# The gate of a feed-forward layer: from one VectorE instruction to one of ScalarE and two of GpSimd, with other block sizes in one pair of batches

## The chip, the core and the metric

The kernel runs on one core of a Trainium2 chip. A core has five engines with queues of their own, each in order: TensorE (PE in the profile; its weight loads are shown apart as PEld), VectorE (DVE), ScalarE (ACT), GpSimd (POOL) and SyncE (SP), which here issues the DMAs. TensorE writes its products to PSUM; the other data lie in SBUF. The metric is the device time of one execution in microseconds, lower being better; a kernel's time is the median of several executions.

## What is computed

Top-k attention, and behind it a feed-forward layer with an ELU gate, on 8 batches of 576 rows and 8 heads of 64:

```python
# attention: q, k, v of (8, 8, 576, 64), float32
scores = scale * np.matmul(q, k.transpose(0, 1, 3, 2))
kth = np.partition(scores, -top_k, axis=-1)[..., -top_k:-top_k + 1]   # top_k = 32
mask = scores >= kth
scores = np.where(mask, scores, -1000000000.0)
scores = scores - np.max(scores, axis=-1, keepdims=True)
attn = np.exp(scores)
attn = attn / (np.sum(attn, axis=-1, keepdims=True) + 1e-09)
attn_out = np.matmul(attn, v)
...
# feed-forward: x is attn_out as (4608, 512); w_in (512, 2048), w_out (2048, 512)
h = x @ w_in
g = np.where(h > 0.0, h, alpha * (np.exp(np.minimum(h, 0.0)) - 1.0))  # alpha = 1
out = g @ w_out
```

The weights come as 64-bit floating-point numbers and are decoded to 32 bits on the core.

## The kernel before

**Tiles and steps.** The 576 query rows of a batch are four tiles of 128 and one of 64; the 64-row tiles of two batches share one slot of the feed-forward layer. So a pair of batches has nine slots of 128 rows. One *step* is one query tile with two heads (for 64-row tiles, four half-filled heads); there are 144 steps, 18 to a batch. The main loop goes over the steps, and what it issues in step n belongs to several of them: `scores` of step n+2, `select` of step n, `mask` and `normalise` of step n-1, `turn` of step n-2, `attend` of a group whose last step is turned.

- `scores` (L273, L281): TensorE multiplies queries by keys into PSUM, ScalarE copies the scaled product to SBUF (`sc`).
- `select` (L291 to L301): for each of the two heads VectorE takes the eight largest values, replaces them by a very small number, and does so until the 32nd largest is known: four MAX8 and three MATCH_REPLACE8 over 576 columns.
- `mask` (L315 to L319): GpSimd makes `neg` and `gap` from the 32nd and the first maximum; ScalarE drops what is under the 32nd with a steep Prelu, and takes Exp, with the sum over a row.
- `normalise` (L328 to L332): GpSimd adds the epsilon (`dene`), VectorE takes the reciprocal (`rec`), GpSimd multiplies the rows.
- `turn` (L348, L349): TensorE transposes the weights into PSUM in two pieces of four 128-column chunks and one of one; ScalarE copies them to `et`. PSUM has two buffers for this and for the products of `attend`.
- `attend` (L375, L399): the product with the values, copied by ScalarE into `xT`, the transposed input of the feed-forward layer. `xT` has two buffers.

**Feed-forward blocks.** Slots are put together in blocks; a block can start when all of its slots are attended. For each of 16 chunks of 128 hidden units, `hidden` multiplies the block's tokens (128, 256 or 384 columns, by the number of slots) with four pieces of `w_in` into a PSUM bank (`hps`, L429). The gate is computed as max(h, exp(min(h, 0)) - 1): ScalarE forms n = Relu(-h) (L437) and n = Exp(-n) (L438), and VectorE takes n - 1 and the maximum with h, from PSUM, in one SCALAR_TENSOR_TENSOR (L409), which writes `gT`. This last instruction is put on a list, `gates`, and issued by `close_gates` at the next call of `feed`, before a third chunk, or before a `project`. Then `project` multiplies a slot's 128 columns of `gT` with `w_out` (L447), in four parts of four matmuls; ScalarE copies the result (L456), and SyncE stores it (L459). `hps` and the product of `project` share two PSUM banks.

**Order of the work.** The pieces of all blocks stand in one list, `ffn`. `feed` is called four times a step and takes pieces off the list at a pace worked out from the blocks' due times: work that must be done before the next block comes is spread evenly. A piece's cost in this sum is `HIDDEN` (by the number of slots) or `PROJECT`. The order on each engine is set when the program is built; the layer that builds it can interleave instructions where their dependencies allow it, so that, for instance, the two heads of a step stand mixed in VectorE's queue. During the first steps `hook` also decodes the weights (L151 to L186), on SyncE, VectorE, ScalarE and GpSimd.

**Divisions.** The first pair of batches has blocks of 1, 1, 2, 1, 2 and 2 slots, the other three pairs of 2, 2, 3 and 2. The 64-row slot (`rest`) lies in the three-slot block.

Of the kernel before, what the change touches and what calls it, by code (L numbers as in the profile page):

```python
# [8 lines left out]
AF = mybir.ActivationFunctionType  # L9
ALU = mybir.AluOpType  # L10
FP32 = mybir.dt.float32
# [4 lines left out]
TAKEN = -1.0e30  # L16
EPS = 1.0e-9
STEEP = 1.0e30
HIDDEN = {1: 1.1, 2: 1.85, 3: 2.7}
PROJECT = 3.55  # L20


# [57 lines left out]
def kernel(  # L80
# [9 lines left out]
    nc = tc.nc  # L90
    P = nc.NUM_PARTITIONS
    B, H, S, D = q.shape
# [8 lines left out]
    NG = NF // 2  # L101
    T = 3 * P
    scale = 1.0 / float(D) ** 0.5
# [3 lines left out]
    def pool(name, bufs, **kw):  # L107
        return ctx.enter_context(tc.tile_pool(name=name, bufs=bufs, **kw))
# [6 lines left out]
    etpool = pool("et", 2)  # L115
    small = pool("small", 4)
    xtpool = pool("xt", 2)
    fpool = pool("f", 2)
    opool = pool("o", 1)
    ps_sc = pool("ps_sc", 1, space=PSUM)  # L120
    ps_t = pool("ps_t", 2, space=PSUM)
# [279 lines left out]
        if blk.left == 0:  # L401
            ffn.extend(ffn_pieces(blk))

    gates = []

    def close_gates():
        for dst, n, ps in gates:
            w = dst.shape[-1]
            nc.vector.scalar_tensor_tensor(  # L409
                out=dst, in0=n[:, 0:w], scalar=-1.0, in1=ps[:, 0:w],  # L410
                op0=ALU.add, op1=ALU.max,
            )
        gates.clear()

    def ffn_pieces(blk):
        n_tok = blk.slots * P

        def hidden(f):
            if f == 0 and blk.number == 0:
                g = early.tile([P, NF, P], FP32, tag="g", name="gT")  # L420
                blk.gT = [g[:, 0:NG], g[:, NG:NF]]
            elif f % NG == 0 and blk.number > 0:
                g = late["g"].tile([P, NG, T], FP32, tag="g", name="gT")
                blk.gT.append(g[:])
            if len(gates) > 1:
                close_gates()
            ps = ps_f.tile([P, dm], FP32, tag="f", name="hps")
            for i in range(NC):
                nc.tensor.matmul(  # L429
                    ps[:, 0:n_tok],  # L430
                    w_in[:, i, f * P : (f + 1) * P],
                    blk.xT[:, i, 0:n_tok],
                    start=(i == 0),
                    stop=(i == NC - 1),
                )
            n = fpool.tile([P, T], FP32, tag="n", name="n")
            nc.scalar.activation(n[:, 0:n_tok], ps[:, 0:n_tok], AF.Relu, scale=-1.0)  # L437
            nc.scalar.activation(n[:, 0:n_tok], n[:, 0:n_tok], AF.Exp, scale=-1.0)  # L438
            gates.append((blk.gT[f // NG][:, f % NG, 0:n_tok], n, ps))

        def project(s, part):
            close_gates()
            if part == 0:
                blk.o = ps_f.tile([P, dm], FP32, tag="f", name="ops")
            step = NF // 4
            for f in range(part * step, (part + 1) * step):
                nc.tensor.matmul(  # L447
                    blk.o[:],
                    blk.gT[f // NG][:, f % NG, s * P : (s + 1) * P],
                    w_out[:, f, :],  # L450
                    start=(f == 0),
                    stop=(f == NF - 1),
                )
            if part == 3:
                o = opool.tile([P, dm], FP32, tag="osb", name="osb")
                nc.scalar.copy(o[:], blk.o[:])  # L456
                for t in blk.tiles[s]:
                    p0 = t.cols.start - s * P
                    nc.sync.dma_start(out[t.rows, :], o[p0 : p0 + t.ql, :])  # L459

        part = HIDDEN[blk.slots]
        behind = 2 * NF if blk.number else 0
        return [
            (part, max(behind, NC * (f // 4 + 1)), lambda f=f: hidden(f))
            for f in range(NF)
        ] + [
            (PROJECT, max(behind, NF + (part + 1) * NF // 4),
             lambda s=s, part=part: project(s, part))
            for s in range(blk.slots)
            for part in range(4)  # L470
        ]
# [4 lines left out]
    for b in range(B):  # L476
        if b % 2 == 0:
            rest = 2 * J
            division = [(0,), (1,), (2, 3), (rest,), (4, 5), (6, 7)]
            if b > 0:  # L480
                division = [(0, 1), (2, 3), (rest, 4, 5), (6, 7)]
            slots = {}
            for part in division:
                blk = Block(len(blocks), len(part))
                blocks.append(blk)
                slots.update((x, (blk, s)) for s, x in enumerate(part))
        first[b] = len(steps)
        tiles = []
        for qt in range(J + 1):
            r0 = b * S + (JP if qt == J else qt)  # L490
            if qt == J:
                (blk, slot), c0, n = slots[rest], (b % 2) * R, R
                rows = slice(r0, r0 + R)
            else:
                (blk, slot), c0, n = slots[(b % 2) * J + qt], 0, P
                rows = slice(r0, r0 + J * (P - 1) + 1, J)
            c0 += slot * P
            t = Tile(b, qt, rows, blk, slice(c0, c0 + n))
            blk.left += NHP
            blk.tiles[slot].append(t)  # L500
            tiles.append(t)
        order = [(0, 1), (2, 3), (J,)] if b % 2 == 0 else [(0, 1), (J,), (2, 3)]
        if b == 0:
            order[:1] = [(0,), (1,)]
        for qts in order:
            for hp in range(NHP // 2 if qts == (J,) else NHP):
                group = Group([tiles[qt] for qt in qts], hp)
                steps += [Step(tiles[qt], hp, group, i) for i, qt in enumerate(qts)]
            for qt in qts:
                n = len(steps)  # L510
                tiles[qt].block.ready = n + 1.0 if n <= tight else n + 2.5
    NS = len(steps)
    total = 0.0
    for blk in sorted(blocks, key=lambda x: x.ready):
        due.append((blk.ready, total))
        total += NF * HIDDEN[blk.slots] + 4 * blk.slots * PROJECT

# [5 lines left out]
    for b in range(1, B):  # L523
        f = first[b]
# [8 lines left out]

    def feed(n, share):

        close_gates()
        fed["at"] = max(fed["at"], n)
        ahead = [(w - fed["sum"]) / (x - fed["at"]) for x, w in due if x > fed["at"]]
        if ahead:
            fed["over"] += max(0.0, share * min(ahead))  # L540
        fed["at"] += share
        while ffn and decoded[0] >= ffn[0][1] and 0.5 * ffn[0][0] <= fed["over"]:
            cost, _, piece = ffn.pop(0)
            fed["over"] -= cost
            fed["sum"] += cost
            piece()
# [26 lines left out]
    for n in range(NS + 3):  # L573
# [5 lines left out]
        if n < tight:  # L579
            for i in range(2):  # L580
                passes = choose(n, i)
                next(passes)
                if i == 0:
                    while closing:
                        attend(closing.pop(0))
                elif prev:
                    normalise(prev)
                    turn(prev, slice(0, J))
                    turn(prev, slice(J, J + 1))
                    turn(prev, slice(J + 1, 2 * J + 1))  # L590
                feed(n, 0.25)
                next(passes)
                mask(cur, i)
                feed(n, 0.25)
            continue
        if prev:
            mask(prev, 0)
        passes = choose(n, 0)
        next(passes)
        feed(n, 0.25)  # L600
        while closing:
            attend(closing.pop(0))
# [15 lines left out]
        feed(n, 0.25)  # L618
    while ffn:
        ffn.pop(0)[2]()  # L620
    close_gates()


# [31 lines left out]
```

## Time and profile before

| what | value |
|---|---|
| median of 5 runs | 1872.49 us (1871.59 to 1872.92) |
| the profiled execution, its own time | 1872.64 us |
| the profiled execution, span of the core | 1870.8 us |
| mean granted TensorE clock | 0.952 |
| VectorE, MAX8 of 576 columns (L291, L301) | 754 and 757 ns, 1152 of them |
| VectorE, MATCH_REPLACE8 (L295) | 749 ns, 864 of them |
| VectorE, gate (L409) by 128, 256, 384 columns | 285, 414, 546 ns; 48, 192, 48 of them |
| ScalarE, Relu from PSUM (L437) by the same | 276, 380, 484 ns |
| ScalarE, Exp (L438) by the same | 310, 416, 524 ns |
| TensorE, passes of `hidden` (L429) by the same | 320, 389, 504 ns; 384, 1536, 384 of them |
| TensorE, passes of `project` (L447) | 606 ns, 1152 of them |

An engine's busy time is the union of its instructions' spans. A float32 matmul stands in the records as two passes; passes overlap, and their ends are modelled, so the mean of one pass is longer than the distance between two in a row. A wait in the profile is idle time of an engine before an instruction, put down to what released it: "A <- B: total us, times, longest". The lists of groups give busy time, mean ns of one, and idle time before them. A row of the windows gives a stretch of the span, then for each engine its busy time and number of instructions, the granted clock, and the DMA's share and rate.

### The profile page before, as it was taken

The page shows a single profiled execution, that of the slowest core. Times are in us where ns is not written, and L with a number is a line of the kernel's source. Part 1 is how long each engine was busy: PE and PEld are TensorE (multiplying, and loading weights), DVE is VectorE, ACT ScalarE, POOL GpSimd, SP SyncE. Part 2 cuts the span into 40 slices and gives each one's busy share as a digit, 9 for nine tenths or more (in the row PEclk, how much of TensorE's full clock was granted, in tenths as well). Part 3 has the DMA queues.
Part 4 walks back from the last instruction along what each step waited for, and adds up shares of the span by engine and source line. Part 5 has one row for each costly group of instructions (what it writes and reads, how often), then busy time and mean ns, then how long its engine had stood idle before and what let it go on. Part 6 is the DMA issues. An engine that isn't in the chain of part 4 may idle for free.

```text
span 1870.8 us, 25844 instructions
## 1 busy us (share of the span) xinstructions
PE 1714.9 (92%) x8352; PEld 1032.6 (55%) x8352; DVE 1605.1 (86%) x3408; ACT 1144.0 (61%) x2505; POOL 442.6 (24%) x1080
## 2 busy tenths in 40 slices
PE   5457999999999999999999999999998999899999
PEld 3235656565665565655546464655546466555555
DVE  7989999999999998989989888988989888898400
ACT  6777667666666665757557575656656565665421
POOL 3776222222222211221221212221221212121100
PEclk8556999999999999999999999999999999999999
DMA  6421011001100101001100011001100000000000
GB/s 162 137 102 68 19 26 45 6 7 47 42 7 1 31 22 47 1 25 27 44 12 1 25 26 44 7 6 38 39 18 7 19 19 26 6 7 6 1 18 12
DMA packets 101126, 56.20 MB, mean 30 GB/s; under 512 B 84096, under 2 KB 92288, under 8 KB 100992
## 3 DMA queue, kind: packets, MB, share of 16 engines
q1 hardware_dynamic: 100992, 54.55, 10.5%
q8 instruction: 67, 1.10, 0.2%
q14 instruction: 67, 0.55, 0.1%
HBM read 45.09 MB, written 9.44 MB: 29 GB/s over the span
## 4 chain that ended last, share of the span: by engine, by line
DVE 61%; PE 21%; ACT 11%; issue 3%; POOL 1%; DMA 1%; SPq 0%; POOLq 0%; ACTq 0%; DVEq 0%
DVE wk L295 25%; DVE m L301 22%; PE hps L429 8%; DVE m L291 8%; PE ops L447 6%; ACT sc L318 3%; DVE gT L409 3%; ACT sc L319 3%; PE scps L273 3%; ACT sc L281 2%; PE avps L375 2%; PE eps L348 2%; DVE raw L168 1%; DMA raw<-in_moe_w_in_dram 1%; DVE raw L182 1%
## 5 line engine op out<-in xcount | busy, mean ns | idle before, releaser
L301 DVE MAX8 m<-wk 128x8 f32<-128x576 f32 x864 | 632.1, 757 | 4.6
L429 PE MATMUL hps<-xT,w_in 128*128 128x256 f32 (+2 forms) x2304 | 576.0, 397 | 38.0 <-DVE gT L409 37.8
L447 PE MATMUL ops<-w_out,gT 128*128 128x512 f32 x1152 | 536.9, 606 | 0.0
L429 PEld LDWEIGHTS hps<-xT,w_in 128*128 128x128 f32 x2304 | 407.9, 198 | 154.3 <-DVE gT L409 59.9
L295 DVE MATCH_REPLACE8 wk<-m,wk 128x576 f32<-128x576 f32 x576 | 430.2, 749 | 0.0
L318 ACT ACTIVATE sc<-sc,neg 128x576 f32<-128x576 f32 x288 | 223.4, 776 | 273.5 <-POOL neg L315 272.2
L447 PEld LDWEIGHTS ops<-w_out,gT 128*128 128x128 f32 x1152 | 209.0, 193 | 207.2 <-issue 201.2
L349 ACT COPY et<-eps 128x512 f32<-128x512 f32 (+1 forms) x432 | 193.5, 475 | 151.5 <-PE eps L348 151.4
L273 PE MATMUL scps<-kqT 64*128 64x64 f32 (+3 forms) x1280 | 258.0, 463 | 14.0 <-ACT sc L281 13.3
L348 PE MATMUL eps<-ident,sc 128*128 128x128 f32 x1296 | 207.9, 284 | 55.2 <-POOL sc L332 17.6
L315 POOL TENSOR_SCALAR neg<-m 128x1 f32<-128x1 f32 x288 | 62.9, 219 | 819.9 <-DVE m L301 819.3
L348 PEld LDWEIGHTS eps<-ident,sc 128*128 128x128 f32 x1296 | 161.1, 145 | 172.0 <-issue 61.3
L332 POOL TENSOR_SCALAR sc<-sc,rec 128x576 f32<-128x576 f32 x288 | 214.2, 754 | 137.9 <-DVE rec L330 132.4
L291 DVE MAX8 m<-sc 128x8 f32<-128x576 f32 x288 | 210.8, 754 | 29.1 <-ACT sc L281 27.2
L319 ACT ACTIVATE sc<-sc,gap 128x576 f32<-128x576 f32 x288 | 223.2, 775 | 16.1 <-ACT sc L318 0.7
L375 PE MATMUL avps<-et,vT 128*64 128x256 f32 (+5 forms) x2000 | 205.8, 338 | 13.7 <-ACT et L349 13.4
L295 DVE MATCH_REPLACE8 wk<-m,sc 128x576 f32<-128x576 f32 x288 | 214.5, 749 | 0.0
L409 DVE SCALAR_TENSOR_TENSOR gT<-n,hps 128x256 f32<-128x256 f32 (+2 forms) x288 | 119.2, 414 | 107.1 <-ACT n L438 105.8
L437 ACT ACTIVATE n<-hps 128x256 f32<-128x256 f32 (+2 forms) x288 | 109.3, 380 | 151.6 <-PE hps L429 150.4
L273 PEld LDWEIGHTS scps<-kqT 64*128 64x128 f32 (+1 forms) x1280 | 117.8, 184 | 136.0 <-issue 112.1
L281 ACT ACTIVATE sc<-scps 128x576 f32<-128x576 f32 x288 | 170.6, 640 | 12.4 <-PE scps L273 12.3
L375 PEld LDWEIGHTS avps<-et,vT 128*64 128x64 f32 (+1 forms) x2000 | 114.4, 140 | 102.9 <-issue 41.1
(38 smaller groups left out, 807.9 us busy)
## 6 DMA issues: line engine op xcount, KB each, us to landing
kin<-in_k_dram SPq DMA_DIRECT2D x64, 128.0 KB, 2.8
qin<-in_q_dram SPq DMA_DIRECT2D x64, 128.0 KB, 2.9
raw<-in_moe_w_in_dram SPq DMA_DIRECT2D x16, 512.0 KB, 4.4
vT<-in_v_dram SPq DMA_DIRECT2D x64, 128.0 KB, 2.3
raw<-in_moe_w_out_dram SPq DMA_DIRECT2D x16, 512.0 KB, 3.2
out_dram<-osb SPq DMA_DIRECT2D x32, 256.0 KB, 2.2
kin<-in_k_dram SPq DMA_DIRECT2D x32, 32.0 KB, 2.5
qin<-in_q_dram SPq DMA_DIRECT2D x32, 32.0 KB, 2.5
```

The lines of the kernel that those rows point to most:

```text
L273: nc.tensor.matmul(ps[rows, start[i] : start[i] + keys.stop - keys.start], kq[part, 1, q0 : q0 + u.t.ql], kq[part, 0, keys], start=True, s ...
L281: nc.scalar.activation(u.sc[:, i, :], ps[:, first[i] : first[i] + S], AF.Copy, scale=scale)
L291: nc.vector.max(m, sc)
L295: nc.vector.match_replace(wk[:], m, cur, TAKEN)
L301: nc.vector.max(m, cur)
L318: nc.scalar.activation(sc, sc, AF.Prelu, bias=neg[:], alpha=STEEP)
L319: nc.scalar.activation(sc, sc, AF.Exp, bias=gap[:], accum_out=u.den[:, i : i + 1])
L332: nc.gpsimd.tensor_scalar(u.sc[:, i, :], u.sc[:, i, :], rec[:, i : i + 1], 1.0, ALU.mult, ALU.mult)
L348: nc.tensor.transpose(ps[:, c * P : (c + 1) * P], sc[:, c0 : c0 + P], ident[:])
L375: nc.tensor.matmul(ps[i * D : (i + 1) * D, cols], vt[rows, 2 * J if c == J else i * J + c, :], w, start=(c == 0), stop=(c == J),)
L429: nc.tensor.matmul(ps[:, 0:n_tok], w_in[:, i, f * P : (f + 1) * P], blk.xT[:, i, 0:n_tok], start=(i == 0), stop=(i == NC - 1),)
L447: nc.tensor.matmul(blk.o[:], blk.gT[f // NG][:, f % NG, s * P : (s + 1) * P], w_out[:, f, :], start=(f == 0), stop=(f == NF - 1),)
```

## The change

VectorE no longer takes part in the gate. The gate is computed as Relu(h) + (Exp(-Relu(-h)) - 1): ScalarE reads the PSUM bank twice, once for Relu(-h) into `n` and once for Relu(h) directly into `gT`, and takes Exp of `n`; GpSimd subtracts one from `n` and adds it to `gT`. `gates` and `close_gates` are gone. The buffer of `n` has three copies instead of two. The pair of batches 4 and 5 is divided into three blocks of three slots; pairs 2-3 and 6-7 keep theirs, as does the first. The costs by which `feed` paces the work are changed for two and three slots.

```diff
-HIDDEN = {1: 1.1, 2: 1.85, 3: 2.7}
+HIDDEN = {1: 1.1, 2: 1.92, 3: 2.68}
...
-    fpool = pool("f", 2)
+    fpool = pool("f", 3)
...
-    gates = []
-
-    def close_gates():
-        for dst, n, ps in gates:
-            w = dst.shape[-1]
-            nc.vector.scalar_tensor_tensor(
-                out=dst, in0=n[:, 0:w], scalar=-1.0, in1=ps[:, 0:w],
-                op0=ALU.add, op1=ALU.max,
-            )
-        gates.clear()
...
-            if len(gates) > 1:
-                close_gates()
...
-            n = fpool.tile([P, T], FP32, tag="n", name="n")
-            nc.scalar.activation(n[:, 0:n_tok], ps[:, 0:n_tok], AF.Relu, scale=-1.0)
-            nc.scalar.activation(n[:, 0:n_tok], n[:, 0:n_tok], AF.Exp, scale=-1.0)
-            gates.append((blk.gT[f // NG][:, f % NG, 0:n_tok], n, ps))
+            n = fpool.tile([P, T], FP32, tag="n", name="n")[:, 0:n_tok]
+            g = blk.gT[f // NG][:, f % NG, 0:n_tok]
+            nc.scalar.activation(n, ps[:, 0:n_tok], AF.Relu, scale=-1.0)
+            nc.scalar.activation(g, ps[:, 0:n_tok], AF.Relu)
+            nc.scalar.activation(n, n, AF.Exp, scale=-1.0)
+            nc.gpsimd.tensor_scalar_add(n, n, -1.0)
+            nc.gpsimd.tensor_tensor(g, g, n, ALU.add)
...
             division = [(0,), (1,), (2, 3), (rest,), (4, 5), (6, 7)]
             if b > 0:
+                division = [(0, 1, 2), (3, 4, 5), (rest, 6, 7)]
+            if b in (2, B - 2):
                 division = [(0, 1), (2, 3), (rest, 4, 5), (6, 7)]
```

The calls of `close_gates` in `project`, in `feed` and at the kernel's end are removed as well.

## The prediction

> **What bounds the kernel now.** I read first the page's busy shares and the chain that ended last, then the engines' busy time by stage, the gate's rows, the waits, and a stretch of the timeline.
>
> ```profile
> PE 1714.9 (92%) x8352; PEld 1032.6 (55%) x8352; DVE 1605.1 (86%) x3408; ACT 1144.0 (61%) x2505; POOL 442.6 (24%) x1080
> ...
> DVE 61%; PE 21%; ACT 11%; issue 3%; POOL 1%; DMA 1%; SPq 0%; POOLq 0%; ACTq 0%; DVEq 0%
> ```
>
> The chain lies mostly on VectorE, yet TensorE is busier. So the stages have to be told apart. I cut the span where the weights are decoded (212 us), where TensorE's load rises (664) and where the last selections end (1741): stages A to D.
>
> ```profile
> 0.00:212.00 212.00, 135.12 (x551) 82.28 (x552) 185.24 (x358) 148.27 (x302) 117.69 (x147) 0.66 0.34 103
> 212.00:664.00 452.00, 437.48 (x2343) 273.92 (x2343) 437.70 (x973) 304.49 (x695) 103.97 (x298) 0.99 0.10 25
> 664.00:1741.00 1077.00, 1017.02 (x5021) 604.92 (x5018) 962.13 (x2035) 657.92 (x1434) 218.52 (x628) 0.99 0.08 20
> 1741.00:1871.00 130.00, 125.28 (x443) 71.52 (x441) 20.08 (x44) 33.33 (x76) 2.43 (x7) 1.00 0.03 11
> ```
>
> Columns after the length: PE, PEld, DVE, ACT, POOL busy. B has both engines at 437 of 452. C has PE at 1017 and DVE at 962 of 1077. D is TensorE alone. The same cut for the gate, L409, on DVE in B and C:
>
> ```profile
> 212.00:664.00 452.00, 32.46 (x88) 0.99 0.10 25
> 664.00:1741.00 1077.00, 71.79 (x161) 0.99 0.08 20
> ```
>
> In A it is 4.35 and in D 10.57 us. The waits of stage C, DVE's and PE's, and two of the whole span:
>
> ```profile
> DVE rec L330 <- POOL dene L328: 64.4, 29, 2.8
> ```
> ```profile
> PE hps L429 <- DVE gT L409: 20.0, 19, 1.9
> ```
> ```profile
> POOL neg L315 <- DVE m L301: 819.3, 267, 8.6
> ...
> ACT sc L318 <- POOL neg L315: 272.2, 161, 5.3
> ```
>
> DVE's 29 waits for `dene` are one loop, seen once in the timeline:
>
> ```profile
> 1259.05 0.76 DVE L301 MAX8 m<-wk 128x8 f32<-128x576 f32 x1
> ...
> 1259.98 0.21 POOL L315 TENSOR_SCALAR neg<-m 128x1 f32<-128x1 f32 x1 [1.95 <-DVE m L301]
> ...
> 1260.22 0.78 ACT L318 ACTIVATE sc<-sc,neg 128x576 f32<-128x576 f32 x1 [0.58 <-POOL neg L315]
> 1261.09 0.78 ACT L319 ACTIVATE sc<-sc,gap 128x576 f32<-128x576 f32 x1
> ...
> 1262.31 0.17 DVE L330 RECIPROCAL rec<-dene 128x2 f32<-128x2 f32 x1 [2.50 <-POOL dene L328]
> ```
>
> The last maximum of a step goes to GpSimd, through ScalarE twice, back to GpSimd and to the reciprocal, which stands next in VectorE's queue: 2.5 us of nothing. So in C VectorE's own side is 962 + 64 = 1026 of 1077, TensorE's 1017. In B they are 437.7 + 2.7 and 437.5 of 452. Two engines are level, and 3 to 5% goes into waiting on each other.
>
> **The change, part by part.**
>
> *Gate off VectorE.* 288 instructions leave (119.2 us in the page's group): 4.4 in A, 32.5 in B, 71.8 in C, all on an engine that sets the pace there; 10.6 in D lies beside TensorE and is worth nothing. The waits of DVE for `n` (13.4 us in C, 10.2 in B) go with them.
>
> *One more Relu on ScalarE.* The blocks of the middle pair become 3+3+3 instead of 2+2+3+2, so hidden chunks are 48 of 128, 144 of 256 and 80 of 384 columns. Priced by the existing Relu from PSUM (0.276, 0.380, 0.484 us):
>
> ```profile
> L437 ACT ACTIVATE n<-hps 128x256 f32<-128x256 f32 x192 | 73.0, 380 | 95.3 <-PE hps L429 95.0
> ```
>
> 13.2 + 54.7 + 38.7 = 107 us; the fewer instructions of the other two give back 6. ACT goes from 1144 to 1245 us, in C from 61 to about 68%. It stays off the limit, but it is in order: behind a Relu stand the mask's Prelu and Exp and the copies that free PSUM for the transposes.
>
> *Two new instructions on GpSimd.* No two-input row of this width exists there. Bounds from these:
>
> ```profile
> L332 POOL TENSOR_SCALAR sc<-sc,rec 128x576 f32<-128x576 f32 x288 | 214.2, 754 | 137.9 <-DVE rec L330 132.4 <-PE qkps L245 1.7 <-PE eps L348 1.3
> ...
> L317 POOL TENSOR_TENSOR gap<-m,m 128x1 f32<-128x1 f32 x288 | 56.7, 197 | 0.4
> ...
> L177 POOL TENSOR_TENSOR raw<-raw 128x512 f32<-128x512 f32 x32 | 43.7, 1366 | 18.2 <-ACT raw L170 18.1
> ```
>
> The scalar add lies between 0.219 us (L315, one column) and 0.754 (576 columns), the tensor add between 0.197 and 1.366. On straight lines between them, by width, a 256-column pair costs 0.45 + 0.78 = 1.23 us; all of them 126 + 221 = 347 us (bounds 113 and 577). I take 347: POOL goes from 443 to 790 us, 42% of the span, and to 55% at the upper bound. It is not the limit either way; it waited 819 us for VectorE alone before `neg`. But it too is in order: `neg`, `gap`, `dene` and the normalising products stand behind the gate, and the gate waits for ScalarE's Exp, which waits for TensorE.
>
> The Trainium skill, GPSIMD Engine Reference, section Engine selection, speaks against this: ordinary elementwise work belongs on VectorE, two-input operations being about twice as slow on GpSimd. The rows agree on the sign (0.414 us for the fused VectorE gate of 256 columns, 1.23 for the pair), and by the rule alone the gate's 119 us would become some 240 and the change a loss of about 120 us, were they on the path (an estimate from that section's factor). I go by where it lies, beside a GpSimd that is idle three quarters of the span.
>
> *PSUM.* A hidden chunk's bank is now free after ScalarE's two Relus instead of after a deferred VectorE instruction. The 20.0 us that PE waits for the gate in C, and 2.8 in B, go; what is late next is ScalarE's second Relu, 0.38 us behind the first, less than the 1.9 us that TensorE works on the next chunk. The third `n` buffer lets GpSimd lag one chunk more.
>
> *Larger blocks.* 384 fewer passes of 256 columns, 256 more of 384. Sixteen in a row take 3.72 and 5.33 us in the timeline: 89 against 85 us. By the mean rows (389 and 504 ns, which overlap) it is 149 against 129. I take nothing; range 0 to -20 us.
>
> *Order.* With the new costs and blocks the built order feeds the network later: counted at these paces, TensorE has done 11 us less of it by step 54 (stage B's end), 27 less by step 88, and is level at step 136. At step 88 the third block of the pair needs the transposed activations' buffer of the first, so 36 hidden matmuls (23 us) stand in one run between two steps' scores. VectorE has two steps (20 us) in hand: price 0 to 15 us, taken 8. The reciprocal stands directly behind the last maximum in 30 steps instead of 31, so the 64 us loop stays. Output and load DMAs are as many as before on SP's queue; the loads are issued seven to one steps ahead, and the one wait of steady work for them is nil in C.
>
> **Sum**, against this execution's span of 1870.8 us (its own time 1872.6, the median shown 1872.5; 1.8 lies around the span).
> A: -4. B: the larger side is now TensorE, 437.5 - 11 = 426 (VectorE 405); with the same 11 us of friction 437, so -15. C: TensorE 1017 + 11 = 1028, VectorE 962 + 64 - 72 = 954. TensorE's idle 60 loses the gate's 20; of the other 40, which are transposes and copies that are late because ScalarE or the normalising was, I let half go, since VectorE is then 7% early where it was level: 1028 + 20 + 8 = 1056, so -21. D: 0. Together -40: 1831 + 1.8, forecast 1833 us. The halving is my choice; its ends are 0 and 40, or -20 and +20 on the time.
>
> **Rivals.**
> 1. *Clean overlap.* Each stage runs at its larger side: B 426, C 1028: -4 - 26 - 49 = -79, 1794 us. For it: part of B is already 99% busy on both. Against: orders are fixed when built, and both engines are never free of each other. 15%.
> 2. *TensorE is the limit and its waits only change names.* ScalarE's longer queue replaces the gate's wait, idle stays: B 452 - 11, C 1077 + 11, burst 8, A -4: 1877 us; with the gate's 20 saved, 1857. For it: 92% busy. 18%, between 1860 and 1880.
> 3. *Slower: the selection's loop grows.* The gate's pair on GpSimd and the Relu on ScalarE (1.23 + 0.38 = 1.6 us) get between last maximum and reciprocal. Over the 131 steps of B and C that is 210 us if all of it counts; it decides once more than 104 / 131 = 0.8 us a step is on the path, half of it. At two thirds, 1.07 us: +140 - 104, 1907 us. For it: ACT already waits 272 us for `neg`. Against: in the built order only 0.4 to 1.1 us of gate a step stands between `neg` and `dene`, while ScalarE works 1.7 us there. 14%.
> 4. *The work does not leave the path at all*, since ScalarE delivers both halves no earlier than now: same time. 3%.
>
> **How the numbers follow.** Forecast (1815 to 1860) 50%, rivals 15, 18, 14 and 3. Beyond 0.2% (3.7 us, about what a measurement of this kernel can tell) faster: 50 + 15 + 11 = 76%; same 7%; slower 17%. The range 1808 to 1884 leaves out half of rival 1 and most of rival 3.
>
> **What would show it.** Right: VectorE near 1486 us busy, POOL near 790, ACT near 1245; no wait of PE for a gate on VectorE; B shorter by 15, C by 21, D unchanged. PE's share rises to 94%. Wrong: if VectorE's wait for `dene` grows well past 64 us, rival 3; if PE's waits for ScalarE's copies grow by what the gate's wait lost, rival 2; if PE idles around step 90 by more than 15 us, the burst was under-priced; if POOL's pair takes over 2 us, so was GpSimd.

## The result, and the profile after

| | before | after |
|---|---|---|
| median (50 and 29 runs) | 1872.67 us | 1877.55 us (1871.67 to 1882.26) |
| ratio, with its 95% interval | | 1.0026 (1.0019 to 1.0033) |
| the profiled execution, own time / span | 1872.64 / 1870.8 us | 1872.33 / 1870.2 us |
| mean granted TensorE clock | 0.952 | 0.947 |

The changed kernel is slower by 0.26%, 4.9 us at the medians (1877.55 us), where 1833 us was forecast. Its profiled execution is among the shortest of its own runs, so the two profiles show equal times; a loss of 5 us can't be read off this pair, but where 40 us of expected gain went can.

Busy shares and chain of the changed kernel:

```profile
PE 1702.0 (91%) x8224; PEld 1003.6 (54%) x8224; DVE 1508.3 (81%) x3120; ACT 1189.8 (64%) x2749; POOL 886.3 (47%) x1624
...
DVE 50%; PE 20%; ACT 17%; POOL 9%; issue 3%; DMA 1%; SPq 0%; ACTq 0%; POOLq 0%; DVEq 0%
```

VectorE lost 97 us, and the span nothing. GpSimd has 886 us where 790 were forecast, and it has entered the chain with 9% (1% before). The stages, cut at the same steps as before (columns as in the prediction):

```profile
0.00:203.00 203.00, 126.55 (x541) 75.42 (x543) 179.51 (x345) 149.15 (x317) 133.44 (x181) 0.66 0.36 108
203.00:648.00 445.00, 423.78 (x2319) 267.57 (x2317) 416.60 (x884) 312.87 (x770) 214.61 (x462) 0.98 0.10 25
648.00:1743.00 1095.00, 1029.12 (x4940) 590.62 (x4937) 902.06 (x1872) 691.48 (x1570) 495.10 (x928) 0.98 0.07 20
1743.00:1871.00 128.00, 122.51 (x434) 70.00 (x432) 10.11 (x21) 36.27 (x96) 43.17 (x54) 0.99 0.03 11
```

A is shorter by 9 us, B by 7, D by 2, and C is longer by 18. The two new instructions by shape (busy, mean ns of one, idle time before):

```profile
L428 POOL TENSOR_SCALAR n<-n 128x256 f32<-128x256 f32 x144 | 123.4, 857 | 123.8 <-ACT n L427 122.3
L429 POOL TENSOR_TENSOR gT<-gT,n 128x256 f32<-128x256 f32 x144 | 105.2, 730 | 10.8
...
L428 POOL TENSOR_SCALAR n<-n 128x384 f32<-128x384 f32 x80 | 94.1, 1176 | 44.6 <-ACT n L427 44.5
L429 POOL TENSOR_TENSOR gT<-gT,n 128x384 f32<-128x384 f32 x80 | 80.1, 1001 | 5.6
```

The subtraction of one, with one input, is slower than the addition of two tensors: 857 ns where the prediction had 450. The addition was priced right (0.78 against 0.73). The waits over the whole span (total, times, longest):

```profile
POOL neg L315 <- DVE m L301: 439.3, 187, 8.5
ACT sc L318 <- POOL neg L315: 292.0, 163, 5.8
...
DVE rec L330 <- POOL dene L328: 112.5, 46, 6.5
DVE m L291 <- ACT sc L281: 106.8, 72, 22.7
...
PE hps L416 <- ACT gT L426: 23.7, 20, 2.3
```

Before, these were 819.3, 272.2, 70.1 and 27.2 us for the first four; for the last, TensorE waited 37.8 us for the gate of VectorE. So the gate's time on VectorE became two other waits of VectorE: for the sum of a row (+42 us) and for the next scores (+80 us). One selection in the changed kernel's timeline:

```profile
1374.81 1.20 POOL L428 TENSOR_SCALAR n<-n 128x384 f32<-128x384 f32 x1 [1.92 <-ACT n L427]
...
1375.97 0.22 POOL L315 TENSOR_SCALAR neg<-m 128x1 f32<-128x1 f32 x1
...
1378.26 1.20 POOL L428 TENSOR_SCALAR n<-n 128x384 f32<-128x384 f32 x1 [0.96 <-ACT n L427]
...
1379.54 0.99 POOL L429 TENSOR_TENSOR gT<-gT,n 128x384 f32<-128x384 f32 x1
1380.62 0.23 POOL L328 TENSOR_SCALAR dene<-den 128x2 f32<-128x2 f32 x1
1380.88 0.17 DVE L330 RECIPROCAL rec<-dene 128x2 f32<-128x2 f32 x1 [6.20 <-POOL dene L328]
```

`neg` stands behind a subtraction in GpSimd's queue, `dene` behind a subtraction and an addition. VectorE waits 6.2 us at the reciprocal.

### The profile page after: what moved, and what is told of

Same layout as the page of the kernel before. It is cut to its first block, busy times and chain, and to the rows that moved or that the text cites. A ratio compares the mean times of both kernels' runs of the same rounds, so it can differ in the third digit from the quotient of the medians.

```text
span 1870.2 us, 25588 instructions
## 1 busy us (share of the span) xinstructions
PE 1702.0 (91%) x8224; PEld 1003.6 (54%) x8224; DVE 1508.3 (81%) x3120; ACT 1189.8 (64%) x2749; POOL 886.3 (47%) x1624
## 3 DMA queue, kind: packets, MB, share of 16 engines
q1 hardware_dynamic: 100992, 54.55, 10.5%
## 4 chain that ended last, share of the span: by engine, by line
DVE 50%; PE 20%; ACT 17%; POOL 9%; issue 3%; DMA 1%; SPq 0%; ACTq 0%; POOLq 0%; DVEq 0%
DVE wk L295 22%; DVE m L301 19%; PE hps L416 7%; PE ops L436 7%; DVE m L291 7%; ACT sc L318 5%; ACT sc L319 4%; POOL n L428 3%; ACT sc L281 3%; POOL gT L429 2%; PE scps L273 2%; PE eps L348 1%; PE avps L375 1%; POOL sc L332 1%; POOL neg L315 1%
## 5 line engine op out<-in xcount | busy, mean ns | idle before, releaser
L416 PE MATMUL hps<-xT,w_in 128*128 128x256 f32 (+2 forms) x2176 | 574.2, 411 | 24.7 <-ACT gT L426 23.7
L416 PEld LDWEIGHTS hps<-xT,w_in 128*128 128x128 f32 x2176 | 386.0, 199 | 143.9 <-ACT gT L426 29.7
L295 DVE MATCH_REPLACE8 wk<-m,wk 128x576 f32<-128x576 f32 x576 | 436.8, 769 | 0.0
L428 POOL TENSOR_SCALAR n<-n 128x256 f32<-128x256 f32 (+2 forms) x272 | 245.3, 902 | 190.0 <-ACT n L427 188.2
L291 DVE MAX8 m<-sc 128x8 f32<-128x576 f32 x288 | 215.4, 774 | 107.6 <-ACT sc L281 106.8
L348 PE MATMUL eps<-ident,sc 128*128 128x128 f32 x1296 | 210.7, 285 | 79.1 <-ACT et L349 27.4
L273 PE MATMUL scps<-kqT 64*128 64x512 f32 (+3 forms) x1280 | 242.6, 464 | 11.4 <-ACT sc L281 10.7
L332 POOL TENSOR_SCALAR sc<-sc,rec 128x576 f32<-128x576 f32 x288 | 214.1, 753 | 75.0 <-DVE rec L330 70.1
L295 DVE MATCH_REPLACE8 wk<-m,sc 128x576 f32<-128x576 f32 x288 | 219.9, 769 | 0.0
L429 POOL TENSOR_TENSOR gT<-gT,n 128x256 f32<-128x256 f32 (+2 forms) x272 | 207.4, 762 | 19.9
L273 PEld LDWEIGHTS scps<-kqT 64*128 64x128 f32 (+1 forms) x1280 | 112.0, 185 | 126.3 <-issue 108.6
```

The source lines that it names most:

```text
L273: nc.tensor.matmul(ps[rows, start[i] : start[i] + keys.stop - keys.start], kq[part, 1, q0 : q0 + u.t.ql], kq[part, 0, keys], start=True, s ...
L291: nc.vector.max(m, sc)
L295: nc.vector.match_replace(wk[:], m, cur, TAKEN)
L332: nc.gpsimd.tensor_scalar(u.sc[:, i, :], u.sc[:, i, :], rec[:, i : i + 1], 1.0, ALU.mult, ALU.mult)
L348: nc.tensor.transpose(ps[:, c * P : (c + 1) * P], sc[:, c0 : c0 + P], ident[:])
L416: nc.tensor.matmul(ps[:, 0:n_tok], w_in[:, i, f * P : (f + 1) * P], blk.xT[:, i, 0:n_tok], start=(i == 0), stop=(i == NC - 1),)
```

## The experiments

Differences are against the runs of the kernel before on the same chip (1872.8 to 1873.4 us).

**The parts of the change alone.**

e1: the changed kernel with the old division of the pair 4 and 5.

```diff
-                division = [(0, 1, 2), (3, 4, 5), (rest, 6, 7)]
-            if b in (2, B - 2):
```

> The new gate with the block division of the kernel before (2, 2, 3 and 2 slots in the middle pair too); the built order then paces the feed-forward work as before did, to within 4 us of TensorE work at every sixth step. Theory A (the blocks of three took the gain: 23 us of hidden matmuls in one run and 27 us of work put off): 1840 to 1855 us. Theory B (TensorE's short waits only changed their names, whoever computes the gate): 1862 to 1875 us. Theory C (GpSimd's pair lies on the path): 1870 us or more.

Measured: 1890.96 us, ratio 1.0100 (1.0084 to 1.0115). The gate alone, as it was written, costs 18 us.

e2: the kernel before with only the new division and paces.

```diff
-HIDDEN = {1: 1.1, 2: 1.85, 3: 2.7}
+HIDDEN = {1: 1.1, 2: 1.92, 3: 2.68}
...
             if b > 0:
+                division = [(0, 1, 2), (3, 4, 5), (rest, 6, 7)]
+            if b in (2, B - 2):
```

> The old gate on VectorE with the new division and the new pacing costs. Theory A: it loses what the blocks cost, 1885 to 1900 us. Theory B: TensorE's total is the same, so within 8 us of before, 1870 to 1880 us. Theory C says nothing of it.

Measured: 1862.81 us, 0.9942 (0.9925 to 0.9959), under every range that was expected. The blocks gain 10 us and hide more than half of the gate's loss. By the page TensorE idles 143 us in this run, its span less its busy time, where it idled 156 before, and it is busy 6 us longer; so the gain is in its waits, not in cheaper passes.

**What of the gate costs.**

e3: the changed kernel without both GpSimd instructions; the gate is then only Relu(h).

```diff
-            nc.gpsimd.tensor_scalar_add(n, n, -1.0)
-            nc.gpsimd.tensor_tensor(g, g, n, ALU.add)
```

> The changed kernel without its two GpSimd instructions (it leaves out the subtraction of one and the adding of the exponential; gT holds Relu(h) alone); TensorE's order is the same. Theory C: 1845 us or less, with VectorE's wait for dene well under 112 us. Theories A and B: 1868 to 1877 us.

Measured: 1846.76 us, 0.9861 (0.9844 to 0.9877), 2 us above theory C's bound and far under the others. The two instructions cost 31 us.

e4: only Relu and Exp on ScalarE, both into `gT`. The second Relu, the subtraction and the sum are left out.

```diff
             nc.scalar.activation(g, ps[:, 0:n_tok], AF.Relu)
-            nc.scalar.activation(n, n, AF.Exp, scale=-1.0)
-            nc.gpsimd.tensor_scalar_add(n, n, -1.0)
-            nc.gpsimd.tensor_tensor(g, g, n, ALU.add)
+            nc.scalar.activation(g, g, AF.Exp, scale=-1.0)
```

> The changed kernel with only two ScalarE instructions as the gate (it leaves out the second Relu, the subtraction and the sum; gT holds Exp(-Relu(h))). Neither VectorE nor GpSimd takes part and ScalarE does no more than before: what a gate at no cost would give with this division. Theory A: 1865 to 1875 us, the blocks still hold it. Theory B: 1860 to 1875 us. Theory C: 1845 us or less.

Measured: 1859.20 us, 0.9932 (0.9915 to 0.9949). It fits no expected range: less work than e3, and 12 us slower. The order on VectorE differs: the reciprocal stands directly behind a step's last maximum in 40 steps (30 in e3). This run can't tell whether that is why, and says nothing of the second Relu's price.

e9: without the subtraction alone (the gate is too large by one).

```diff
-            nc.gpsimd.tensor_scalar_add(n, n, -1.0)
```

> The changed kernel without the subtraction of one on GpSimd (gT is too large by one everywhere); the tensor add stays, and now is the one that waits for ScalarE's Exp. Theory C by GpSimd's time: 245 of the pair's 453 us go, so 245/453 of the 31 us that leaving out both gave: 1857 to 1866 us. If what counts is that GpSimd's queue waits for Exp at all, not how long it works: 1870 to 1877 us.

Measured: 1849.96 us, 0.9877 (0.9864 to 0.9890). Nearly the whole loss hangs on the subtraction; the addition without it costs 3 us (against e3). That is less time than either range expected, so the cost does not go by an instruction's share of GpSimd's time.

e5: the same sum in another form. In the kernel before, the normalising product has a second operation that changes nothing (times 1.0), and takes 754 ns for 576 columns, less than the new subtraction for 256.

```diff
-            nc.gpsimd.tensor_scalar_add(n, n, -1.0)
+            nc.gpsimd.tensor_scalar(n, n, -1.0, 1.0, ALU.add, ALU.mult)
```

> The changed kernel with the subtraction of one written with a second operation (add -1, then multiply by 1), the form in which the normalising product runs at 1.3 ns a column where the single add ran at 3.1. If the form sets the speed, 256 columns take 0.35 to 0.5 us instead of 0.86; theory C by GpSimd's time then gives 1862 to 1870 us. If the two-operation form is as slow, 1873 to 1880 us.

Measured: 1846.73 us, 0.9866 (0.9850 to 0.9882): all that leaving out both instructions had gained, and 15 us under the expected range. Its rows of the subtraction:

```profile
L428 POOL TENSOR_SCALAR n<-n 128x256 f32<-128x256 f32 x144 | 58.1, 403 | 133.1 <-ACT n L427 132.9
...
L428 POOL TENSOR_SCALAR n<-n 128x384 f32<-128x384 f32 x80 | 40.9, 511 | 61.2 <-ACT n L427 61.0
```

403 ns instead of 857, 511 instead of 1176. Their starts say the same: at 256 columns the addition starts 487 ns after the subtraction instead of 942 (medians, where the addition comes next). The order on every engine is the same as in the changed kernel, so this is a pure test of one duration. The selection shown above, in e5's timeline:

```profile
1357.67 0.51 POOL L428 TENSOR_SCALAR n<-n 128x384 f32<-128x384 f32 x1 [1.92 <-ACT n L427]
1358.14 0.21 POOL L315 TENSOR_SCALAR neg<-m 128x1 f32<-128x1 f32 x1
...
1360.74 0.51 POOL L428 TENSOR_SCALAR n<-n 128x384 f32<-128x384 f32 x1 [1.29 <-ACT n L427]
...
1361.34 1.00 POOL L429 TENSOR_TENSOR gT<-gT,n 128x384 f32<-128x384 f32 x1
1362.42 0.23 POOL L328 TENSOR_SCALAR dene<-den 128x2 f32<-128x2 f32 x1
1362.68 0.17 DVE L330 RECIPROCAL rec<-dene 128x2 f32<-128x2 f32 x1 [5.14 <-POOL dene L328]
```

From the first subtraction to the reciprocal it is 5.01 us instead of 6.07.

g1: e1 in e5's form (the gate alone, written well).

> e1_gate_alone (new gate, division of the kernel before) with the subtraction in the two-operation form of e5_other_form. If the single-operation form alone made the new gate slow, its 30 us go here too: 1855 to 1866 us, which is what the new gate by itself is worth against before. If the blocks of three were needed to make room for it: 1875 us or more.

Measured: 1862.29 us, 0.9945 (0.9931 to 0.9959). So the gate is worth 10.5 us and the blocks 10; together 26. The slow form takes back 31 with the new blocks and 29 without (e1 less g1).

In both pairs, the changed kernel and e5, e1 and g1, the order on every engine is the same and the form of one instruction is all that differs. The busy shares of e5, then e1, then g1:

```profile
PE 1686.1 (91%) x8224; PEld 993.8 (54%) x8224; DVE 1508.6 (82%) x3120; ACT 1189.2 (64%) x2749; POOL 753.2 (41%) x1624
...
PE 1712.2 (91%) x8352; PEld 1035.9 (55%) x8352; DVE 1512.2 (80%) x3120; ACT 1190.8 (63%) x2793; POOL 893.8 (47%) x1656
...
PE 1691.7 (91%) x8352; PEld 1024.6 (55%) x8352; DVE 1512.3 (81%) x3120; ACT 1190.9 (64%) x2793; POOL 761.6 (41%) x1656
```

VectorE and ScalarE are as busy as with the slow form. TensorE is not: for the same passes it is busy 16 us longer in the changed kernel than in e5 (1702.0 against 1686.1) and 20.5 longer in e1 than in g1, and in both pairs it idles some 10 us more (span less busy time). In the first pair most of that idle time is before the transposes of the weights (`eps`, 79.1 us against 73.4), the rest before those of keys and queries and before `hidden`. The longer busy time is taken up in the last section.

q1: e5 with a further fast instruction that adds nothing, so that GpSimd's queue per chunk is again nearly as long (1.53 us at 256 columns, 2.02 at 384; the changed kernel 1.59 and 2.18).

```diff
+            nc.gpsimd.tensor_scalar(n, n, 0.0, 1.0, ALU.add, ALU.mult)
```

> e5_other_form with a further add of zero in the two-operation form behind the subtraction: GpSimd's part of the gate is then three instructions of 0.40 + 0.40 + 0.73 us at 256 columns, as long as the changed kernel's 0.86 + 0.73. If the time that GpSimd works in its queue is the cost: 1868 to 1880 us, like the changed kernel. If the single-operation form does something else to the other engines: 1845 to 1855 us.

Measured: 1864.60 us, 0.9955 (0.9944 to 0.9967). Neither range had it: 18 of the 31 us come back with a longer queue of fast instructions. GpSimd is busy 865 us in it (e5 753, changed kernel 886), so its queue got 84% of the time and 58% of the loss. TensorE's order is the changed kernel's; VectorE's and ScalarE's differ from it in a few places.

Together these runs show a price that sets in late. GpSimd is busy 443 us in e3, 642 in e9, 753 in e5, 865 in q1 and 886 in the changed kernel, and the times are 1846.8, 1850.0, 1846.7, 1864.6 and 1877.6 us: the first 310 us of added work cost nothing that can be told, the last 133 cost 31.

d5: the changed kernel with the reciprocal left out (rows are multiplied by their sum instead).

```diff
-        rec = small.tile([P, 2], FP32, tag="rec", name="rec")
-        nc.vector.reciprocal(rec[:], den[:])
+        rec = den
```

> The changed kernel without VectorE's reciprocal (it leaves out the division: rows are multiplied by their sum), so VectorE never waits for dene; all other engines do the same work. Theory D (VectorE's 112 us of waiting for dene set the time): 1835 to 1850 us. Theory C: the gate's pair still delays the products and the mask, 1862 to 1877 us.

Measured: 1873.31 us, 1.0002 (0.9991 to 1.0014). VectorE's wait for `dene` (112 us) is gone, and 4 us are gained (against 1877.55; the order on all engines also differs in places). What VectorE waits for instead:

```profile
DVE m L291 <- ACT sc L281: 193.6, 69, 27.9
```

The next scores, 194 us where it was 107. By this run the wait for `dene` is worth some 4 us, not 112; the scores come when TensorE gets to them.

**Who sets the pace.**

v1: the kernel before with one more MAX8 of 576 columns a step on VectorE (144 of 0.75 us, 108 us).

```diff
+        if i == 0:
+            spare = small.tile([P, 8], FP32, tag="spare", name="spare")
+            nc.vector.max(spare[:], sc)
```

> The kernel before with one more MAX8 a step on VectorE (108 us). The prediction took VectorE as level with TensorE there: then 1940 to 1980 us. If TensorE sets the pace there too: 1875 to 1900 us.

Measured: 1877.76 us, 1.0025 (1.0013 to 1.0038). The added durations sum to 108 us and cost 4.4. Its busy shares and its chain:

```profile
PE 1708.8 (91%) x8352; PEld 1031.9 (55%) x8352; DVE 1679.5 (89%) x3552; ACT 1144.6 (61%) x2505; POOL 440.2 (23%) x1080
...
DVE 69%; PE 16%; ACT 9%; issue 3%; POOL 2%; DMA 1%; SPq 0%; POOLq 0%; ACTq 0%; DVEq 0%
```

VectorE's share of the chain rose from 61 to 69%, and the span by 7 us. That share tells whose instructions the chain ran through, not whose time the span follows. VectorE's busy time rose by 74 us, not 108, because the records of neighbouring instructions overlap: the extra MAX8 takes 745 ns, and the next instruction starts 660 ns after it. The built order also moves with this edit, as it does in s1 and s2, so each price is that of the edit as a whole.

s1: the same edit on e5.

> e5_other_form with one more MAX8 of 576 columns a step on VectorE, into a spare tile (144 x 0.75 = 108 us of VectorE work). If TensorE sets the pace and VectorE has room: 1847 to 1870 us, up to a fifth of it. If the engines are level, as the prediction had it for the kernel before: 1890 us or more.

Measured: 1852.50 us, 0.9892 (0.9880 to 0.9905): 6 us for 108 (72 of busy time).

s2: e5 with one more matmul of 128 columns for each hidden chunk on TensorE (544 passes; 60 us, an estimate from the 0.11 us between two passes of that width in a row).

```diff
+            nc.tensor.matmul(
+                ps[:, 0:P],
+                w_in[:, 0, f * P : (f + 1) * P],
+                blk.xT[:, 0, 0:P],
+                start=True,
+                stop=True,
+            )
```

> e5_other_form with one more matmul of 128 columns in each hidden chunk on TensorE, overwritten by the next (272 x 2 passes x 0.111 = 60 us of TensorE work). If TensorE sets the pace: 1895 to 1912 us, nearly all of it. If the engines are level: 1865 to 1885 us.

Measured: 1926.74 us, 1.0293 (1.0277 to 1.0309): 80 us for 60, more than was expected. By the page TensorE is busy 70 us longer than in e5 and idles 10 more. TensorE sets the pace.

From the traces I took for each step when TensorE begins its scores, and how long after that VectorE begins to select it (us):

```
step    before       after        e5           v1
  12    201 / 11.0   195 /  7.8   193 /  8.6   191 / 19.9
  24    310 / 34.6   304 / 15.2   303 / 15.4   312 / 45.3
  36    451 / 16.5   435 /  3.8   431 /  3.9   455 / 34.2
  54    660 /  3.6   644 /  4.4   633 /  4.4   669 / 21.9
  72    872 /  4.5   853 /  3.6   841 /  3.6   881 /  8.6
  90   1090 /  3.4  1057 /  4.9  1041 /  5.0  1098 /  4.2
 114   1377 /  7.3  1358 /  6.1  1341 /  6.1  1383 /  7.9
 143   1737         1735         1711         1744
 end   1871         1870         1845         1878
```

From step 54 on VectorE starts 3 to 8 us behind the scores in the kernel before too: it keeps up with TensorE. Between steps 12 and 36 it is up to 35 us behind, and in v1 45, and catches up later; TensorE arrives at step 143 only 7 us later in v1.

**Versions that might be faster.**

h1: e2, with the changed gate (slow form) only in the blocks of the first pair, where VectorE falls behind.

```diff
+            if blk.number < 6:
+                m, g = n[:, 0:n_tok], blk.gT[f // NG][:, f % NG, 0:n_tok]
+                nc.scalar.activation(m, ps[:, 0:n_tok], AF.Relu, scale=-1.0)
+                nc.scalar.activation(g, ps[:, 0:n_tok], AF.Relu)
+                nc.scalar.activation(m, m, AF.Exp, scale=-1.0)
+                nc.gpsimd.tensor_scalar_add(m, m, -1.0)
+                nc.gpsimd.tensor_tensor(g, g, m, ALU.add)
+                return
```

> Blocks of the first pair of batches (their hidden work is done by about step 46) with the new gate, all later blocks with the old one on VectorE; division and pacing as in the changed kernel. Theory C (the new gate gains while VectorE sets the pace, 28 us by step 36, and GpSimd's pair costs more than that once TensorE sets it): 1863 us of e2_blocks_alone less some 20 to 28, so 1835 to 1845 us, step 36 near 440 us. Theory B (TensorE's waits only change their names): 1858 to 1868 us, the early gain is paid back whoever computes the later gates.

Measured: 1859.39 us, 0.9928 (0.9915 to 0.9942): 3 us under e2, in theory B's range. TensorE begins step 36 12 us earlier than in e2 (434 and 446), but step 54 only 3 us earlier (644 and 647). Of what the early gate gains, almost nothing lasts in this run.

g2: e5 with three blocks of three slots in the pair 2 and 3 too.

```diff
-            if b in (2, B - 2):
+            if b == B - 2:
```

> e5_other_form with blocks of 3, 3 and 3 slots in batches 2 and 3 too. If blocks of three help by themselves (e2_blocks_alone gained 10 us): 1836 to 1845 us. If the run of 23 us of hidden matmuls at each such pair costs what the larger blocks save: 1844 to 1856 us.

Measured: 1844.22 us, 0.9854 (0.9839 to 0.9869), the same as e5 within the intervals. e5 and g2 beat both kernels.

b1 and b2: e5 with copies moved from ScalarE to VectorE, b1 those of the transposed queries and keys, b2 that of `xT`.

```diff
-            nc.scalar.copy(d[:, i, 0:JP], ps[:])
+            nc.vector.tensor_copy(d[:, i, 0:JP], ps[:])
...
-        nc.scalar.copy(
+        nc.vector.tensor_copy(
             d[:, :, JP:S], ps[:, 0 : 2 * R].rearrange("p (a s) -> p a s", a=2)
         )
...
-        nc.scalar.copy(blk.xT[:, at, cols], src)
+        nc.vector.tensor_copy(blk.xT[:, at, cols], src)
```

> e5_other_form with the copies of the transposed keys and queries (64 of 512 and 32 of 128 columns) on VectorE instead of ScalarE. If TensorE's waits for ScalarE's copies are what is left to win and VectorE has room: 1835 to 1844 us. If the copies come later behind MAX8 than behind ScalarE's queue: 1846 us or more.

> e5_other_form with the copies into xT (88 of 64 to 256 columns) on VectorE. If ScalarE's lateness is what TensorE waits for: 1836 to 1844 us; if VectorE's queue is later: 1846 us or more.

Measured: 1860.41 us, 0.9932 (0.9915 to 0.9949), and 1849.35 us, 0.9871 (0.9854 to 0.9889). b1 loses 14 us against e5, b2 gains nothing. The copies came later: TensorE waits 49 us for `xT` in b2 and 13 in e5, and in b1 its wait for the normalising product before the transposes grows from 26 to 49 us. What a shorter queue on ScalarE alone would be worth is not shown.

## Why the prediction was wrong, point by point

**The step that failed first is a term of the sum: "a 256-column pair costs 0.45 + 0.78 = 1.23 us; all of them 126 + 221 = 347 us".** The pair took 857 + 730 ns at 256 columns, 1176 + 1001 at 384, 453 us in all, inside the stated bounds (113 to 577); the sign named for this, a pair of over 2 us, appeared at 384 columns (2.18). The tensor add was right, the scalar add off by 1.9 and 2.1 times. The straight line ran from one column (0.219) to 576 columns (0.754), and the row at its far end has two operations; the one at the near end is too short to show what a column costs. In the two-operation form the line's values (0.45 and 0.57) are a little above what e5 shows (0.403 and 0.511). So the price was near for another spelling of the instruction, and the difference was worth 30.8 us (changed kernel against e5). The measured time is 44.6 us above the forecast; with the fast form, at 1846.73 us, 13.7 us of it remain, and these belong to the steps below.

**"POOL goes from 443 to 790 us ... It is not the limit either way."** True, and the wrong question: the sum put its delay at nothing. At 47% busy it delays, for it is in order, and `neg` and `dene` stand behind the gate. Of the 31 us, q1 reproduces 18 with a longer queue alone. The rest is open: the changed kernel's queue is 0.06 to 0.16 us a chunk longer than q1's, both reach step 114 within 1 us of each other (1358 and 1357), and they part from there to step 120 (79 and 73 us), where VectorE's built order differs a little. This is rival 3's place, the gate's pair between the last maximum and the reciprocal, at under a quarter of its price: it put two thirds of 1.6 us a step on the path (140 us); 31 us over the 131 steps are 0.24 us a step. The sign it named, a wait for `dene` well past 64 us, appeared (92 in stage C), but it tells little: over the whole span this wait is 112 us in the changed kernel, 97 in e5 and 94 in e3, which has no gate on GpSimd, and without it d5 gains 4 us. What GpSimd delays is felt where TensorE waits, in the changed kernel against e5 mostly at the transposes.

**"Two engines are level."** This premise failed. By busy time they were (VectorE 1026 of 1077 with its wait, TensorE 1017), by price not: 108 us more on VectorE cost 4 (v1, the kernel before) and 6 us (s1), 60 us more on TensorE cost 80 (s2, on e5). "On an engine that sets the pace there" was thus wrong for the 104 us taken off VectorE in B and C. The row that could have told was in the trace before: VectorE began a step 34.6 us behind its scores at step 24 and 3.6 at step 54, so it was the faster of the two in between and followed TensorE from there on. Only in the early steps was VectorE's load worth something: in g1, the gate alone, TensorE begins step 54 15 us earlier than in the kernel before (645 and 660) and step 143 11 us earlier (1726 and 1737), so the 10.5 us of the gate come before step 54 and nothing after it.

Rival 2, TensorE is the limit and its waits only change names, had the right engine and much of the mechanism. TensorE's idle time did not fall (156 us before, 168 after): its wait for the gate fell from 37.8 to 23.7 us, its waits for ScalarE's copies grew from 85 to 95, and those for GpSimd from 23 to 36. But its 1877 was measured by luck, since it put the time down to ScalarE's queue: e5 has the same instructions on ScalarE in the same order and takes 1847.

**The stages.** With the well-written instruction, e5 shows what the rest of the sum was worth:

```profile
201.00:638.00 437.00, 417.73 (x2321) 263.12 (x2319) 417.28 (x887) 312.55 (x770) 183.31 (x464) 1.00 0.10 25
638.00:1717.00 1079.00, 1021.18 (x4937) 586.63 (x4932) 901.61 (x1871) 690.75 (x1568) 410.16 (x928) 0.99 0.08 20
```

B is 15 us shorter than before, as forecast, but by luck: TensorE is busy 418 us in it, not 426, and idles 19, not 11. (The 11 was VectorE's idle time; TensorE's in the row before is 14.5.) A is 11 us shorter (4 were forecast), D 2 (0). C is 2 longer, where 21 shorter were forecast. The 11 us of feed-forward work that move from B to C were there (9 us by step 54, level by step 143). What wasn't there was the fall of TensorE's idle time, the gate's 20 and, of "the other 40", the half that the sum "let go": it is 60 us in C before and 58 in e5, where the sum had 28, and 156 and 158 over the whole span. The reason given, that VectorE is 7% early, falls with the premise, and so does rival 1's clean overlap (1794 us), which no run came near. TensorE's share, forecast at 94%, is 91.

**The burst, 8 us.** The delay was larger: VectorE's steps 90 to 96 took 99 us instead of 74, the next six 58 instead of 69, a net 14. The 22.7 us in the waits above is this place. But e2 and e5 have the same steps (98 and 99 us, then 58) and are 10 and 26 us faster than the kernel before, so no run shows that it costs time.

**Larger blocks, "I take nothing; range 0 to -20".** e2 gives 10, the middle of the range. It is TensorE's idle time that fell, and why was not isolated.

**ScalarE and VectorE.** VectorE came to 1508 us (1486 forecast) and ScalarE to 1190 (1245 forecast), so ScalarE's busy time rose by under half of the 101 us that were added up. The prediction summed durations, and neighbouring records overlap: the second Relu of 256 columns takes 386 ns, and the next instruction starts 264 ns after it (median). The forecast time did not rest on either.

**The skill's rule that was weighed.** The Trainium skill, GPSIMD Engine Reference, section Engine selection, was set aside in the prediction because GpSimd was mostly idle. The sign of its advice held for the instruction as it was written (e1, +18 us) and not for the other form (g1, -10.5). The rule calls two-input operations about twice as slow there and one-input ones roughly at line rate. From 128 to 384 columns VectorE's gate takes 1.0 ns a column, GpSimd's two-input addition 2.1 and the two-operation subtraction 0.75, which agrees; the one-operation subtraction takes 2.3, which does not.

## What to carry to other kernels

Two engines that are equally busy aren't equally limiting: add a known amount of work to each, or follow how far the consumer starts behind the producer, before an edit is priced on one of them. An engine at half load can still delay what stands in order behind the new work: here 310 us more on GpSimd cost nothing and the next 133 cost 31, so the added duration counts once the small instructions of the main loop that pass through it come too late. And price an instruction from a row of the same form, the number of its operations included; writing it in the form whose row is known was worth 31 us here.

## What the hardware showed that was not expected

**A one-operation scalar add on GpSimd is slower than the same add with a second operation that does nothing**: 578, 857 and 1176 ns against 318, 403 and 511 at 128, 256 and 384 columns of float32. From 256 to 384 columns that is 2.5 against 0.84 ns a column. Why is not shown by these runs.

**A short stop of TensorE can be followed by half clock.** Three neighbouring stretches of the changed kernel (length, then TensorE's busy time and passes first, granted clock third from the end):

```profile
1005.50:1009.10 3.60, 1.46 (x9) 1.03 (x8) 3.60 (x10) 3.60 (x12) 2.09 (x4) 1.00 0.00 0
1009.10:1012.50 3.40, 3.40 (x9) 1.90 (x9) 3.37 (x7) 1.22 (x4) 3.14 (x5) 0.50 0.00 0
1012.50:1015.90 3.40, 3.40 (x24) 2.38 (x22) 3.39 (x8) 2.61 (x7) 1.93 (x4) 1.00 0.00 0
```
```profile
1008.02 0.66 PE L348 MATMUL eps<-ident,sc 128*128 128x128 f32 x4 [2.14 <-ACT et L349]
1008.52 3.04 PE L416 MATMUL hps<-xT,w_in 128*128 128x256 f32 x8
```

TensorE is idle for about 2.1 us, waiting for ScalarE's copy of `et`; soon after, its granted clock is 0.50 for 3.4 us, and eight passes of `hidden` take 3.04 us (1.99 for eight just before the stop). Such windows mostly last 3.4 or 6.8 us. I counted the changed kernel's distances between the starts of two passes (2.5 us at this place) after the first 212 us, and those with a window that begins within 4.5 us of the distance's start: none of 23 between 1 and 1.5 us, 1 of 13 between 1.5 and 2, 4 of 8 between 2 and 2.5, and 10 of 12 above. The Trainium skill, TensorE: Matmul & The Clock Gate, section HAM oscillation, asks for no idle gaps of TensorE above about 3.4 us; here half of the distances of 2 to 2.5 us were already followed by half clock.

After the first 212 us, the profiled executions hold this much time at half clock: e3 24 us, e5 31, before 38, e2 44, q1 and g1 48, changed kernel 61, e1 89. If half of such a window is lost, (61 - 31) / 2 = 15 us of the 25.6 between the profiled executions of the changed kernel and of e5 stand under this head, and 20 of the 31 between e1 and g1. TensorE's busy time in that stretch bears it out: it is 15 and 19 us longer, for the same passes in the same order. Some 10 more are idle time in each pair. No run held the clock fixed, so what the stops would cost without it is not shown. It would also be why s2's 60 us cost 80 (58 us at half clock against 31 in e5, so 14 of the other 20), but that is argued from the same sum and not shown.

Left open: the 13 us between q1 and the changed kernel (9.5 between their profiled executions, of which the clock's share is (61 - 48) / 2 = 7); why TensorE idles less with the larger blocks; and why e4 is slower than e3.
